# Rebuilding weight sums from copies in DRAM, two softmax units at a time, in an attention and gated-projection kernel on one Trainium2 core

## The chip, the core and the metric

The kernel runs on one core of a Trainium2 chip. The metric is the device time of one execution in microseconds (us). The engines are named as the profile names them: PE is TensorE (PEld its weight loads), DVE is VectorE, ACT is ScalarE, POOL is GpSimd, and SP is SyncE, which issues most DMAs; PEq, ACTq, SPq are the sequencers of the engines.

## The reference

Attention over 4 batches, 8 heads, 768 positions, head size 64, with a window of 128 and 4 sink positions that every row sees; then a gated projection with two weights of 512 x 1536 and one of 1536 x 512:

```python
scores = scale * np.matmul(q, k.transpose(0, 1, 3, 2))
keep = is_sink | in_window
scores = np.where(keep, scores, -1000000000.0)
scores = scores - np.max(scores, axis=-1, keepdims=True)
a = np.exp(scores)
a = a / (np.sum(a, axis=-1, keepdims=True) + 1e-09)
x = np.matmul(a, v)              # to rows of 512, 3072 of them
return (x @ w_a) * (x @ w_b) @ w_out
```

The weights arrive as 64-bit floats. The kernel computes at close to fp32 accuracy: an fp32 operand is split into a high part, rounded for fast matmuls (fp32r), and a low part, the rest; a product is three matmuls: high by high, high by low, low by high.

## The kernel before, in words

**Chunks.** The 3072 rows are done in seven chunks. The first holds the first tile of 128 rows of each batch (512 rows), the second and third the second tiles of two batches each (256 rows), and the fourth to seventh the remaining four tiles of a batch each (512 rows). While the projection of one chunk runs, the attention of the next runs beside it. In the profile, the first chunk takes about 0 to 168 us, the second to 248, the third to 322, the three following some 117 us each, the last to the end.

**First chunk (`first_tiles`, then `moe`).** Here the 36 weight tiles `w_a`, `w_b`, `w_o` (12 of each, `[128, 512]`) are loaded as 64-bit words (L340), turned into fp32 in an `io` buffer (`wf`: L347, L348 on DVE, L356 on ACT, L359 on DVE, for the first three on POOL), rounded to the high part by ACT (L371) and subtracted to the low part by DVE (L377). `moe` runs over 12 steps j: product with `w_a` (L892), copy on ACT (L927), product with `w_b`, DVE multiplication (L931), high part on ACT (L934), low part on DVE (L936), and the projection with `w_o` of the step before (L919). Beside it runs the exact attention of the second chunk: scores (L800), subtraction and maximum on DVE (L804), exponential on ACT (L806), sums (L809, L810), scaling (L811), transposes (L823), eviction of the transposed probabilities (L824), product with v (L834). In this chunk the instructions not marked by `keep_in_program_order` are ordered by the list scheduler.

**Second and third chunk (`moe2`).** The same 12 steps for 256 rows (L976 to L983), in slots: three per step, 37 calls in the second chunk. A slot runs the step's own operations, advances the attention by its pace (`PACE`), runs one stage of each piece of deferred work (`later`, `step_late`). From the second chunk on, PE, DVE, ACT and POOL keep the order in which the code was written (`begin_order`, `keep_order`); SP's DMAs don't. The attention beside the second chunk is at first the exact one of the third chunk (`apart`), then the split one for whole batches (keys and queries split on POOL, L404 and L407; scores L695; L701, L702 on DVE; exponential L704 on ACT; sums L711, L712 on DVE; scaling L713 and the copy of the sink columns L714 on ACT).

**Later chunks (`moe7`).** The products with `w_a` and `w_b` are done by halves with seven products instead of eight, which needs four sums S1 to S4 of the halves of two neighbouring tiles (2i and 2i + 1), split into high and low. These are built once, by `convert`, for i = 0 to 5 and both weights: twelve times, called rebuilds here. A rebuild adds the high and low parts of the two tiles back to fp32 (L1013, L1014), makes the four sums on POOL (L1017, L1018, L1021, L1022, each `[128, 256]`), rounds on ACT (L1025), subtracts on DVE (L1031), and sends the two results to DRAM with `send` (L1040, 512 KB each), whence `fetch` streams them in the later chunks (L1054).

**Where the rebuilds stand.** Six stand in the first chunk's steps 1 to 6 (`behind(j)`; the sums with `e = gpsimd`, their tiles in the homes of weights that come late, `LATE_HOMES`), four in the second chunk at slots 0, 8, 15 and 22 (in the tile `xh`, sums on DVE) and two in the third at slots 12 and 22 (in `w_o1`, `w_o2`):

```python
CONVERTS = {1: (0, 8, 15, 22), 2: (12, 22)}
LATE_HOMES = (("w_o11", "w_o10"), ("w_b11", "w_a11"))
return [[sums], [first], [second], [lambda: high(0)], [lambda: high(1), lambda: low(0)], [lambda: low(1)]]
```

In the split attention every unit (a head and a tile) ends on its own in `finish`, at the slot after its exponential:

```python
nc.vector.tensor_scalar(st[:, 2:3], st[:, 1:2], 1e-9, None, op0=ALU.add)
nc.vector.reciprocal(st[:, 3:4], st[:, 2:3])
nc.scalar.mul(p, p, st[:, 3:4])
nc.scalar.copy(sc[i][:, h, :], p[:, P:])
```

Other transfers that matter: keys and queries of the split attention (L427, L431), the exact attention's loads (L789 to L792), rows of the output (L1191), copies of `w_o` to DRAM (`send_o`). `io` is a ring of six buffers of `[128, 512]`.

Of the kernel before, what the change touches and what calls it, by code (L numbers as in the profile page):

```python
# [19 lines left out]
DM, FF = 512, 1536  # L20
# [217 lines left out]
class Fast:  # L238
# [419 lines left out]
    def parts_split(self, segs):  # L658
# [31 lines left out]
        def scores(h, i):  # L690
            ks, qh, ql = kq[h]
            u = f"{tag}_{h}_{i}"
            ps = self.ps.tile([P, SW], F32, tag=self.bank("s"), name=f"s{u}")
            for n, q in enumerate((qh, ql)):
                nc.tensor.matmul(ps, lhsT=q[:, i * P:(i + 1) * P], rhs=ks[:, c0s[i]:c0s[i] + SW],  # L695
                                 start=n == 0, stop=n == 1)
            if i % 2 == 0:
                state["p"] = self.at.tile([P, 2, W], F32, tag="p", name=f"p{u}")
            p = state["p"][:, i % 2, :]
            st = self.at.tile([P, 4], F32, tag="st", name=f"st{u}", bufs=8)  # L700
            nc.vector.copy_predicated(ps[:, :P], self.own.bitcast(mybir.dt.uint16), ps[:, W:])  # L701
# [3 lines left out]
            state[h, i] = p, st  # L705
            if h == 0:
                sc[i] = self.at.tile([P, H, NS], F32, tag=f"sc{i}", name=f"sc{u}", bufs=2)

        def finish(h, i):
            p, st = state[h, i]  # L710
            nc.vector.tensor_scalar(st[:, 2:3], st[:, 1:2], 1e-9, None, op0=ALU.add)  # L711
            nc.vector.reciprocal(st[:, 3:4], st[:, 2:3])  # L712
            nc.scalar.mul(p, p, st[:, 3:4])  # L713
            nc.scalar.copy(sc[i][:, h, :], p[:, P:])  # L714

        def transposes(h):
            tp = self.ps.tile([P, nt, P], F32, tag=self.bank("t"), name=f"t{tag}_{h}")
            for i in range(nt):
                nc.tensor.transpose(tp[:, i, :], state.pop((h, i))[0][:, :P], self.ident)  # L719
# [20 lines left out]
        def sinks_t():  # L740
# [3 lines left out]
            for i in range(nt):  # L744
                nc.tensor.transpose(tp[:, i * P:(i + 1) * P], sc[i].rearrange("p a b -> p (a b)"), self.ident)
# [16 lines left out]
    def parts_exact(self, segs, xf, apart):  # L762
# [56 lines left out]
        def transposes(h, i):  # L819
# [4 lines left out]
            nc.scalar.copy(ptx[:, h % 2, 2 * i:2 * i + 2, :], tp)  # L824
# [123 lines left out]
    def moe2(self, c, rows, xs, between, extra):  # L948
# [23 lines left out]
        for j in range(NJ):  # L972
# [8 lines left out]
            self.later([[lambda g=g, gh=gh: A.copy(gh, g)],  # L981
                        [lambda e=e, g=g, gh=gh, gl=gl: e.tensor_tensor(gl, g, gh.bitcast(F32), op=ALU.subtract)]])  # L982
# [13 lines left out]
    def convert(self, kind, i, homes, e):  # L996

        nc = self.nc
        (eh, el), (oh, ol) = self.wt[kind, 2 * i], self.wt[kind, 2 * i + 1]
        tag = f"{kind}{i}"  # L1000
        g, flat = nc.gpsimd, lambda x: x.rearrange("p a c -> p (a c)")
        f, h, q = None, None, None

        def sums():
            nonlocal f, h, q
            if homes is None:
                both = self.mo.tile([P, 8, HK], F32, tag="xh", name=f"s_{tag}", bufs=1)
                f, h = both[:, :4], both[:, 4:].bitcast(F32R)
            else:
                f = self.wp.tile([P, 4, HK], F32, tag=homes[0], name=f"sf_{tag}")  # L1010
                h = self.wp.tile([P, 4, HK], F32R, tag=homes[1], name=f"sh_{tag}")
            q = [f[:, k, :] for k in range(4)]
            e.tensor_tensor(flat(f[:, :2]), oh.bitcast(F32), ol.bitcast(F32), op=ALU.add)  # L1013
            e.tensor_tensor(flat(f[:, 2:]), eh.bitcast(F32), el.bitcast(F32), op=ALU.add)  # L1014

        def first():
            g.tensor_tensor(q[1], q[0], q[1], op=ALU.add)  # L1017
            g.tensor_tensor(q[0], q[2], q[0], op=ALU.subtract)  # L1018

        def second():  # L1020
            g.tensor_tensor(q[2], q[1], q[2], op=ALU.subtract)  # L1021
            g.tensor_tensor(q[3], q[3], q[2], op=ALU.subtract)  # L1022

        def high(k):
            nc.scalar.copy(flat(h[:, 2 * k:2 * k + 2]), flat(f[:, 2 * k:2 * k + 2]))  # L1025
            if k:
                self.send(("H", kind, i), flat(h).bitcast(F32))

        def low(k):
            x = flat(f[:, 2 * k:2 * k + 2])  # L1030
            nc.vector.tensor_tensor(x.bitcast(F32R), x, flat(h[:, 2 * k:2 * k + 2]).bitcast(F32), op=ALU.subtract)  # L1031
            if k:
                self.send(("L", kind, i), flat(f))

        return [[sums], [first], [second], [lambda: high(0)], [lambda: high(1), lambda: low(0)], [lambda: low(1)]]

    def send(self, key, x):
        d = self.away[key] = self.dr.tile([P, 2 * DM], F32, tag="d_" + "_".join(map(str, key)),
                                          name="d_" + "_".join(map(str, key)))
        self.nc.sync.dma_start(d, x)  # L1040
# [278 lines left out]
    def run(self, scalars, verdict):  # L1319
# [56 lines left out]
        for c in range(len(chunks) + 1):  # L1376
# [33 lines left out]
            def behind(j):  # L1410
                if 1 <= j < 7:
                    i, k = (j - 1) // 2, (j - 1) % 2
                    for part in self.convert("ab"[k], i, LATE_HOMES[k], self.nc.gpsimd):
                        for f in part:
                            f()

            def send_o(j):
                self.send(("O", j), self.whole["o", j].bitcast(F32).rearrange("p a c -> p (a c)"))

            def extra(s):  # L1420
                j, k = divmod(s, 3)
                if c == 1:
                    if s in CONVERTS[1]:
                        n = 6 + CONVERTS[1].index(s)
                        yield self.convert("ab"[n % 2], n // 2, None, self.nc.vector)
# [5 lines left out]
                if s in CONVERTS[2]:  # L1431
                    n = 10 + CONVERTS[2].index(s)
                    yield self.convert("ab"[n % 2], n // 2, ("w_o1", "w_o2"), self.nc.vector)
# [110 lines left out]
```

## Time and profile before

| | us |
|---|---|
| median of 3 runs | 782.2 (781.09 to 784.73) |
| profiled execution | 781.96 |
| its span, first to last instruction | 780.2 |
| PE busy | 738.4 (95%) |
| DVE busy | 474.9 (61%) |
| ACT busy | 415.6 (53%) |
| POOL busy | 395.5 (51%) |

A row of a table by stage gives, for a stretch of the span, the time that each engine was busy in it (and its instructions), the mean TensorE clock that was granted (PEclk, 1.00 is full speed), the mean busy share of the 16 DMA engines and what they moved. A row of a list of groups gives line, engine, operation, what is written and read, the count, then busy time and mean length of one (ns), then the idle time of the engine just before them and what ended it. In a timeline the number in brackets is the idle time before the instruction and its releaser. Lengths of overlapping instructions include the overlap.

### The profile page before, as it was taken

Reading aid. Unit: us, or ns where it says so; the run is one execution under the profiler, and the core shown is the slowest. Engines: PE = TensorE matmul, PEld = TensorE weight load, DVE = VectorE, ACT = ScalarE, POOL = GpSimd, SP = SyncE. Lnnn points to the kernel's source line nnn. Section 1 sums busy time; section 2 is a strip of 40 time slices with the busy share of each in tenths; the row PEclk is TensorE's granted clock in tenths of the full one; section 3 lists DMA queues with packets and bytes.
Section 4 is the critical chain, followed back from the end, with each engine's and each line's share of the span. In section 5 each row is a group of like instructions: output and inputs, shape, how many; then the busy total and the mean of one; then the engine's idle time right before and its main releaser. Section 6 shows DMA issues by size and latency. Waiting matters only on the chain.

```text
span 780.2 us, 14687 instructions
## 1 busy us (share of the span) xinstructions
PE 738.4 (95%) x4952; PEld 646.4 (83%) x4952; DVE 474.9 (61%) x1397; ACT 415.6 (53%) x1215; POOL 395.5 (51%) x402
## 2 busy tenths in 40 slices
PE   9887969999988999889999999999999999999997
PEld 6765748788877989888988898888898888889896
DVE  6899989945446565765564665564665664543322
ACT  6575557647646664566652476652475552444211
POOL 2646430022285673577753877753877733533340
PEclk9998989999999999999999999999999999999999
DMA  9875747535432444377876577776576765589551
GB/s 337 307 253 206 258 151 264 214 120 165 139 118 92 128 138 163 129 247 222 252 246 227 179 264 252 255 246 218 187 272 240 244 214 198 198 290 332 188 163 57
DMA packets 70275, 163.27 MB, mean 209 GB/s; under 512 B 7473, under 2 KB 24881, under 8 KB 70193
## 3 DMA queue, kind: packets, MB, share of 16 engines
q1 hardware_dynamic: 70048, 162.26, 61.8%
q8 instruction: 41, 0.67, 0.3%
q14 instruction: 42, 0.34, 0.1%
q10 hardware_dynamic: 144, 0.00, 0.0%
HBM read 138.64 MB, written 23.59 MB: 208 GB/s over the span
## 4 chain that ended last, share of the span: by engine, by line
PE 76%; DVE 8%; POOL 7%; ACT 3%; issue 3%; DMA 2%; SPq 0%; ACTq 0%; DVEq 0%; POOLq 0%
PE o L1181 15%; PE a L892 6%; PE b L892 6%; PE av L731 4%; PE s L695 4%; PE o L969 4%; PE o L919 3%; PE t L719 2%; PE X_1b L1134 2%; PE X_4b L1134 2%; PE X_2b L1134 2%; PE X_3b L1134 2%; PE s L800 2%; PE X_0b L1134 2%; PE X_4a L1134 1%
## 5 line engine op out<-in xcount | busy, mean ns | idle before, releaser
L1181 PE MATMUL o<-r_O,gh 128*128 128x512 f32 x288 | 93.7, 406 | 0.0
L1294 POOL TENSOR_TENSOR gl<-bu,gh 128x512 fp32r<-128x512 f32 x46 | 59.3, 1289 | 54.2 <-ACT gh L1291 53.3
L713 ACT ACTIVATE p<-p,st 128x132 f32<-128x132 f32 x128 | 52.0, 406 | 54.1 <-DVE st L712 53.9
L704 ACT ACTIVATE p<-p,st 128x132 f32<-128x132 f32 x128 | 51.9, 405 | 53.6 <-DVE st L702 53.1
L711 DVE TENSOR_SCALAR st<-st 128x1 f32<-128x1 f32 x128 | 19.4, 152 | 64.2 <-ACT p L704 64.2
L701 DVE COPY_PREDICATED s<-own,s 128x128 f32<-128x128 uint16 x128 | 36.9, 288 | 34.5 <-PE s L695 33.9
L1181 PE MATMUL o<-r_O,gl 128*128 128x512 f32 x144 | 56.5, 392 | 0.0
L407 POOL TENSOR_TENSOR ks<-kr,ks 64x656 fp32r<-64x656 f32 x32 | 50.9, 1592 | 2.7
L1181 PEld LDWEIGHTS o<-r_O,gh 128*128 128x128 f32 x288 | 45.0, 189 | 2.6 <-issue 2.1
L1227 POOL TENSOR_TENSOR bu<-x 128x256 f32<-128x256 f32 x24 | 19.0, 792 | 53.8 <-DVE x L1226 53.6
L919 PE MATMUL o<-w_o,gh 128*128 128x512 f32 x96 | 35.0, 436 | 9.4 <-DVE w_o L377 8.2
L721 DVE TENSOR_TENSOR pt<-t,tri 128x1024 f32<-128x1024 f32 x32 | 39.1, 1221 | 6.1 <-PE t L719 6.1
L982 POOL TENSOR_TENSOR gl<-g,gh 128x256 fp32r<-128x256 f32 x22 | 18.2, 828 | 48.4 <-ACT gh L981 48.2
L407 POOL TENSOR_TENSOR ql<-qr,qh 128x512 fp32r<-128x512 f32 x32 | 41.3, 1292 | 1.5
L892 PE MATMUL a<-x,w_a 128*128 128x256 f32 x288 | 41.0, 292 | 0.4 <-DVE x L877 0.4
L404 POOL TENSOR_SCALAR ks<-kr 64x656 fp32r<-64x656 f32 x32 | 23.9, 746 | 34.1 <-PE s L695 33.5
L695 PE MATMUL s<-ks,qh 128*128 128x260 f32 x128 | 37.9, 296 | 3.3 <-DVE st L702 2.0
L702 DVE CUSTOM_DVE_ANT_0 p<-s,mg 128x132 f32<-128x132 f32 x128 | 37.8, 296 | 4.4
L1291 ACT CAST gh<-bu 128x512 fp32r<-128x512 f32 x48 | 29.5, 614 | 19.5 <-PE o L1181 10.2
L892 PE MATMUL b<-x,w_b 128*128 128x256 f32 x288 | 39.4, 285 | 0.0
L892 PEld LDWEIGHTS a<-x,w_a 128*128 128x128 f32 x288 | 37.8, 195 | 1.3 <-DVE x L877 0.6
L695 PE MATMUL s<-ks,ql 128*128 128x260 f32 x128 | 36.6, 286 | 1.0 <-POOL ql L407 1.0
(495 smaller groups left out, 2327.4 us busy)
## 6 DMA issues: line engine op xcount, KB each, us to landing
r_O<-d_O SPq DMA_DIRECT2D x36, 512.0 KB, 4.4
r_H_a<-d_H_a SPq DMA_DIRECT2D x24, 512.0 KB, 5.2
r_L_a<-d_L_a SPq DMA_DIRECT2D x24, 512.0 KB, 6.0
r_H_b<-d_H_b SPq DMA_DIRECT2D x24, 512.0 KB, 5.0
r_L_b<-d_L_b SPq DMA_DIRECT2D x24, 512.0 KB, 5.7
qr<-in_qT_dram SPq DMA_DIRECT2D x32, 256.0 KB, 3.4
raw_a<-in_wa_dram SPq DMA_DIRECT2D x12, 512.0 KB, 6.4
raw_b<-in_wb_dram SPq DMA_DIRECT2D x12, 512.0 KB, 5.3
```

The costliest lines, as they stand in the source:

```text
L407: self.nc.gpsimd.tensor_tensor(o, i, high.bitcast(F32), op=ALU.subtract)
L695: nc.tensor.matmul(ps, lhsT=q[:, i * P:(i + 1) * P], rhs=ks[:, c0s[i]:c0s[i] + SW], start=n == 0, stop=n == 1)
L701: nc.vector.copy_predicated(ps[:, :P], self.own.bitcast(mybir.dt.uint16), ps[:, W:])
L702: nc.vector.tensor_tensor_reduce(out=p, in0=ps[:, :W], in1=self.mg[:, :W], scale=-0.125, scalar=BIG, op0=ALU.add, op1=ALU.min, accum_out=s ...
L704: nc.scalar.activation(p, p, AF.Exp, bias=st[:, 0:1], scale=-1.0, accum_out=st[:, 1:2])
L713: nc.scalar.mul(p, p, st[:, 3:4])
L721: nc.vector.tensor_tensor(self.parted(nt)[:, h % 2].rearrange("p (c m) q -> p c m q", m=2), tp.unsqueeze(2).to_broadcast(shape), self.tri. ...
L892: mm = self.nc.tensor.matmul(ps[:, cols], lhsT=w[:, ksl], rhs=x[:, kk, cols], start=start and kk == 0 and i == 0, stop=kk == NK - 1 and i ...
L919: nc.tensor.matmul(outs[i], lhsT=g[:, sl], rhs=w, start=j == 0 and k == 0, stop=j == NJ - 1 and k == 2)
L1134: mm = self.nc.tensor.matmul(ps, lhsT=a[:, ksl], rhs=b[:, kk, :], start=start and kk == 0 and n == 0, stop=kk == 1 and n == 2, skip_group_ ...
L1181: self.nc.tensor.matmul(outs[t], lhsT=g[:, sl], rhs=w, start=j == 0 and n == 0, stop=j == NJ - 1 and n == 2)
L1294: (V if late else G).tensor_tensor(hl[k][1], halves[k], hl[k][0].bitcast(F32), op=ALU.subtract)
```

## The change

1. The fp32 values of each `w_a` and `w_b` tile are stored to DRAM when the tile is made in the first chunk: 24 DMAs of 256 KB on ACT's queue, behind the high part.
2. No rebuild stands in the first chunk. Seven stand in the second (slots 0 to 24, alternately in `xh` and in four `io` buffers) and five in the third (slots 12 to 26, in tiles of `w_o`).
3. A rebuild loads the two fp32 tiles (two DMAs of 256 KB on SP) where it added high and low parts before; its POOL operations start two slots later. Its results are sent in halves: four stores of 256 KB where there were two of 512 KB.
4. In the split attention two units share a `p` and an `st` tile, and `finish` runs once for both.
5. The exact attention of the third chunk evicts the transposed probabilities on DVE where ACT did it.
6. In `moe2` the last step's low part `gl` is made in the same slot as its high part.

```diff
-CONVERTS = {1: (0, 8, 15, 22), 2: (12, 22)}
+CONVERTS = {1: ((0, "xh"), (3, "io"), (8, "xh"), (11, "io"), (16, "xh"), (19, "io"), (24, "xh")),
+            2: ((12, ("w_o1", "w_o2")), (18, ("w_o3", "w_o4")), (20, ("w_o1", "w_o2")), (23, ("w_o5", "w_o6")),
+                (26, ("w_o3", "w_o4")))}
-LATE_HOMES = (("w_o11", "w_o10"), ("w_b11", "w_a11"))
@@ weight_high
         self.tc.keep_in_program_order(self.nc.scalar.copy(w[:, 0, :], self.wf[kind, j]))
+        if kind != "o":
+            self.send(("F", kind, j), self.wf[kind, j], self.nc.scalar)
@@ parts_split: scores, finish
             if i % 2 == 0:
                 state["p"] = self.at.tile([P, 2, W], F32, tag="p", name=f"p{u}")
+                state["st"] = self.at.tile([P, 4, 2], F32, tag="st", name=f"st{u}", bufs=8)
-            st = self.at.tile([P, 4], F32, tag="st", name=f"st{u}", bufs=8)
+            st = state["st"][:, :, i % 2]
...
         def finish(h, i):
+            if i % 2 == 0:
+                return
             p, st = state[h, i]
-            nc.vector.tensor_scalar(st[:, 2:3], st[:, 1:2], 1e-9, None, op0=ALU.add)
-            nc.vector.reciprocal(st[:, 3:4], st[:, 2:3])
-            nc.scalar.mul(p, p, st[:, 3:4])
-            nc.scalar.copy(sc[i][:, h, :], p[:, P:])
+            nc.vector.tensor_scalar(st[:, 2], st[:, 1], 1e-9, None, op0=ALU.add)
+            nc.vector.reciprocal(st[:, 3], st[:, 2])
+            for k in range(2):
+                nc.scalar.mul(p[:, k, :], p[:, k, :], st[:, 3, k:k + 1])
+            nc.scalar.copy(sc[0][:, i - 1:i + 1, h, :], p[:, :, P:])
@@ parts_exact: transposes
-            nc.scalar.copy(ptx[:, h % 2, 2 * i:2 * i + 2, :], tp)
+            (nc.vector.tensor_copy if apart else nc.scalar.copy)(ptx[:, h % 2, 2 * i:2 * i + 2, :], tp)
@@ moe2
-            self.later([[lambda g=g, gh=gh: A.copy(gh, g)],
-                        [lambda e=e, g=g, gh=gh, gl=gl: e.tensor_tensor(gl, g, gh.bitcast(F32), op=ALU.subtract)]])
+            parts = [[lambda g=g, gh=gh: A.copy(gh, g)],
+                     [lambda e=e, g=g, gh=gh, gl=gl: e.tensor_tensor(gl, g, gh.bitcast(F32), op=ALU.subtract)]]
+            self.later(parts if j < NJ - 1 else [parts[0] + parts[1]])
@@ convert
-            e.tensor_tensor(flat(f[:, :2]), oh.bitcast(F32), ol.bitcast(F32), op=ALU.add)
-            e.tensor_tensor(flat(f[:, 2:]), eh.bitcast(F32), el.bitcast(F32), op=ALU.add)
+        def fetch():
+            if homes == "io":
+                f[:] = [self.io([P, 2, HK], F32, f"sf{k}_{tag}") for k in range(2)]
+                h[:] = [self.io([P, 2, HK], F32R, f"sh{k}_{tag}") for k in range(2)]
+            else:
...
+            for k in range(2):
+                nc.sync.dma_start(f[k].rearrange("p a c -> p (a c)"), self.away["F", kind, 2 * i + 1 - k])
...
+        def part(n, x, k):
...
+            nc.sync.dma_start(self.away[key][:, k * DM:(k + 1) * DM], x.rearrange("p a c -> p (a c)"))
...
-        return [[sums], [first], [second], [lambda: high(0)], [lambda: high(1), lambda: low(0)], [lambda: low(1)]]
+        return [[fetch], [], [first], [lambda: high(0), second], [lambda: high(1), lambda: low(0)], [lambda: low(1)]]
@@ run
             def behind(j):
-                if 1 <= j < 7:
-                    i, k = (j - 1) // 2, (j - 1) % 2
-                    for part in self.convert("ab"[k], i, LATE_HOMES[k], self.nc.gpsimd):
-                        for f in part:
-                            f()
+                pass
```

## Rows read from the trace of the kernel before

**Rows 1.** The page, busy time of each engine over the span

```profile
PE 738.4 (95%) x4952; PEld 646.4 (83%) x4952; DVE 474.9 (61%) x1397; ACT 415.6 (53%) x1215; POOL 395.5 (51%) x402
```

**Rows 2.** Table by stage: PE, PEld, DVE, ACT, POOL busy; PEclk, DMA share, GB/s

```profile
0.00:24.00 24.00, 22.28 (x175) 17.66 (x176) 16.35 (x54) 16.53 (x47) 5.62 (x22) 1.00 0.93 331
24.00:105.00 81.00, 64.04 (x297) 48.78 (x297) 76.75 (x132) 47.39 (x100) 47.69 (x38) 0.91 0.67 231
105.00:168.00 63.00, 63.00 (x300) 49.75 (x301) 53.30 (x118) 36.58 (x83) 0.37 (x1) 0.98 0.57 197
168.00:248.00 80.00, 75.66 (x527) 67.33 (x526) 37.92 (x149) 48.27 (x148) 38.43 (x43) 0.96 0.42 137
248.00:322.00 74.00, 69.70 (x519) 62.34 (x519) 46.01 (x147) 45.03 (x140) 42.22 (x46) 1.00 0.41 131
322.00:434.00 112.00, 109.80 (x801) 99.12 (x801) 68.25 (x237) 60.06 (x197) 69.76 (x70) 1.00 0.73 239
```

**Rows 3.** Chain of waits that ended last, 24 to 168 us: start, length, what

```profile
86.40 4.12 DMA d_L_b<-sf_b
90.67 1.81 POOL sf_b L1013
...
104.80 3.62 PE o L919 x8
```

**Rows 4.** PE's waits, 24 to 105 us: total, times, longest

```profile
PE o L919 <- DVE w_o L377: 8.2, 3, 6.3
PE s L800 <- DVE st L804: 3.8, 1, 3.8
```

**Rows 5.** Table by stage of L348, L359 (DVE, then POOL), L347 alone, in turn

```profile
24.00:105.00 81.00, 17.92 (x18) 0.91 0.67 231
105.00:165.00 60.00, 11.01 (x16) 0.97 0.60 206
...
24.00:105.00 81.00, 15.66 (x17) 3.03 (x2) 0.91 0.67 231
105.00:165.00 60.00, 11.00 (x16) 0.00 (x0) 0.97 0.60 206
...
24.00:105.00 81.00, 12.31 (x18) 0.91 0.67 231
105.00:165.00 60.00, 6.40 (x16) 0.97 0.60 206
```

**Rows 6.** Table by stage of L1031 alone (DVE)

```profile
24.00:105.00 81.00, 7.88 (x9) 0.91 0.67 231
```

**Rows 7.** ACT's timeline at the start: its only DMA issue

```profile
0.81 0.40 ACTq L1474 DMA_DIRECT2D nw_raw<-in_nw_dram  x1
```

**Rows 8.** Groups of POOL by line, 168 to 320 us: a rebuild's operation

```profile
L1018 POOL TENSOR_TENSOR s_a<-s_a 128x256 f32<-128x256 f32 x2 | 1.5, 738 | 0.2
```

**Rows 9.** The page's DMA issues: count, KB each, us from issue to landing

```profile
out_dram<-os SPq DMA_DIRECT2D x24, 256.0 KB, 2.9
```

**Rows 10.** PE's timeline in the second and third chunk

```profile
224.62 0.58 PE L695 MATMUL s<-ks,ql 128*128 128x260 f32 x1 [0.96 <-POOL ql L407]
...
244.75 0.79 PE L969 MATMUL o<-w_o,gl 128*128 128x512 f32 x1 [1.90 <-DVE gl L982]
...
283.06 0.50 PE L969 MATMUL o<-w_o,gl 128*128 128x512 f32 x1 [1.94 <-POOL gl L982]
...
320.55 0.50 PE L969 MATMUL o<-w_o,gl 128*128 128x512 f32 x1 [1.93 <-DVE gl L982]
```

**Rows 11.** Waits of SP's queue, 160 to 320 us: total, times, longest

```profile
SPq L427 <- POOL ks L407: 31.1, 4, 11.3
```

**Rows 12.** Groups by line: the split attention's sums over the span; evictions, 168 to 320 us

```profile
L711 DVE TENSOR_SCALAR st<-st 128x1 f32<-128x1 f32 x128 | 19.4, 152 | 64.2 <-ACT p L704 64.2
L712 DVE RECIPROCAL st<-st 128x1 f32<-128x1 f32 x128 | 21.1, 164 | 4.4
...
L824 ACT COPY ptx<-t 128x256 f32<-128x256 f32 x16 | 5.7, 357 | 0.1
```

More of the change, by code (lines that the diff above doesn't have):

```diff
@@ L994, in moe2, with convert @@
             self.store(outs[t], r, t, f"{c}_{t}", False)
-    def convert(self, kind, i, homes, e):
+    def convert(self, kind, i, homes):
         nc = self.nc
-        (eh, el), (oh, ol) = self.wt[kind, 2 * i], self.wt[kind, 2 * i + 1]
         tag = f"{kind}{i}"
[L1001 to L1008, printed above, removed]
-            else:
-                f = self.wp.tile([P, 4, HK], F32, tag=homes[0], name=f"sf_{tag}")
-                h = self.wp.tile([P, 4, HK], F32R, tag=homes[1], name=f"sh_{tag}")
-            q = [f[:, k, :] for k in range(4)]
-            e.tensor_tensor(flat(f[:, :2]), oh.bitcast(F32), ol.bitcast(F32), op=ALU.add)
-            e.tensor_tensor(flat(f[:, 2:]), eh.bitcast(F32), el.bitcast(F32), op=ALU.add)
+        g = nc.gpsimd
+        f, h = [], []
+        def fetch():
+            if homes == "io":
+                f[:] = [self.io([P, 2, HK], F32, f"sf{k}_{tag}") for k in range(2)]
+                h[:] = [self.io([P, 2, HK], F32R, f"sh{k}_{tag}") for k in range(2)]
+            else:
+                if homes == "xh":
+                    both = self.mo.tile([P, 8, HK], F32, tag="xh", name=f"s_{tag}", bufs=1)
+                    x, y = both[:, :4], both[:, 4:].bitcast(F32R)
+                else:
+                    x = self.wp.tile([P, 4, HK], F32, tag=homes[0], name=f"sf_{tag}")
+                    y = self.wp.tile([P, 4, HK], F32R, tag=homes[1], name=f"sh_{tag}")
+                f[:], h[:] = ([t[:, 2 * k:2 * k + 2] for k in range(2)] for t in (x, y))
+            for k in range(2):
+                nc.sync.dma_start(f[k].rearrange("p a c -> p (a c)"), self.away["F", kind, 2 * i + 1 - k])
+        q = lambda k: f[k // 2][:, k % 2, :]
@@ L1016, in first @@
         def first():
[L1017 to L1018 removed]
+            g.tensor_tensor(q(1), q(0), q(1), op=ALU.add)
+            g.tensor_tensor(q(0), q(2), q(0), op=ALU.subtract)
         def second():
[L1021 to L1022 removed]
+            g.tensor_tensor(q(2), q(1), q(2), op=ALU.subtract)
+            g.tensor_tensor(q(3), q(3), q(2), op=ALU.subtract)
@@ L1024, in high @@
+        def part(n, x, k):
+            key = (n, kind, i)
+            if key not in self.away:
+                self.away[key] = self.dr.tile([P, 2 * DM], F32, tag="d_" + "_".join(map(str, key)),
+                                              name="d_" + "_".join(map(str, key)))
+            nc.sync.dma_start(self.away[key][:, k * DM:(k + 1) * DM], x.rearrange("p a c -> p (a c)"))
         def high(k):
-            nc.scalar.copy(flat(h[:, 2 * k:2 * k + 2]), flat(f[:, 2 * k:2 * k + 2]))
-            if k:
-                self.send(("H", kind, i), flat(h).bitcast(F32))
+            nc.scalar.copy(h[k], f[k])
+            part("H", h[k].bitcast(F32), k)
@@ L1029, in low @@
         def low(k):
[L1030 to L1033, printed above, removed]
-        return [[sums], [first], [second], [lambda: high(0)], [lambda: high(1), lambda: low(0)], [lambda: low(1)]]
-    def send(self, key, x):
-        d = self.away[key] = self.dr.tile([P, 2 * DM], F32, tag="d_" + "_".join(map(str, key)),
+            nc.vector.tensor_tensor(f[k].bitcast(F32R), f[k], h[k].bitcast(F32), op=ALU.subtract)
@@ L1039, in send @@
+            part("L", f[k], k)
+        return [[fetch], [], [first], [lambda: high(0), second], [lambda: high(1), lambda: low(0)], [lambda: low(1)]]
+    def send(self, key, x, queue):
+        d = self.away[key] = self.dr.tile(list(x.shape), F32, tag="d_" + "_".join(map(str, key)),
                                           name="d_" + "_".join(map(str, key)))
-        self.nc.sync.dma_start(d, x)
+        queue.dma_start(d, x)
     def shift(self, i):
@@ L1410, in behind @@
             def behind(j):
-                if 1 <= j < 7:
-                    i, k = (j - 1) // 2, (j - 1) % 2
-                    for part in self.convert("ab"[k], i, LATE_HOMES[k], self.nc.gpsimd):
-                        for f in part:
-                            f()
+                pass
             def send_o(j):
-                self.send(("O", j), self.whole["o", j].bitcast(F32).rearrange("p a c -> p (a c)"))
+                self.send(("O", j), self.whole["o", j].bitcast(F32).rearrange("p a c -> p (a c)"), self.nc.sync)
             def extra(s):
                 j, k = divmod(s, 3)
+                for n, (at, homes) in enumerate(CONVERTS[c], len(CONVERTS[1]) * (c - 1)):
+                    if at == s:
+                        yield self.convert("ab"[n % 2], n // 2, homes)
                 if c == 1:
-                    if s in CONVERTS[1]:
-                        n = 6 + CONVERTS[1].index(s)
-                        yield self.convert("ab"[n % 2], n // 2, None, self.nc.vector)
                     if k == 0 and j < KEPT:
```

13 lines of the change are left out of this document (5 added, 8 removed).

## The prediction

> **What bounds the kernel now.** I read the page first: TensorE (PE) is busy for 738.4 of 780.2 us, so the whole kernel can give back little more than 42 us of idle PE, plus what PE loses at a lower clock [rows 1]. The table by stage says where those 42 us lie: 17.0 of them between 24 and 105 us, inside the first chunk, where the granted clock averages 0.91. From 105 to 168 us PE has no gap. The second and third chunk lose 4.3 us each, and the stage from 322 to 434 us, which stands for three alike, loses 2.2 [rows 2].
>
> The chain of waits then says what PE waits for from 24 to 105 us. It runs through VectorE (DVE) and through GpSimd (POOL), which rebuilds weight sums there: a store of an earlier rebuild (4.1 us) lets POOL start L1013 at 90.7 us, then come eleven POOL operations one after another, and PE goes on at 104.8 us [rows 3]. In the list of PE's waits the low halves of w_o (L377, on DVE) cost 8.2 us and one wait for the score subtraction on DVE 3.8, together 12.0 of the 17.0 [rows 4]. The stage table shows that DVE is busy for 76.75 of these 81 us: it is DVE that is late.
>
> Why DVE is late is seen by putting its lines in the two stretches side by side. L348 takes 17.92/18 = 1.00 us in the first and 11.01/16 = 0.69 in the second, L359 0.92 against 0.69, L347 0.68 against 0.40 [rows 5]. The operations are the same; what differs is POOL, busy for 47.69 us in the first stretch and 0.37 in the second [rows 2]. [...]
>
> **The change, part by part.**
>
> *The first chunk loses six rebuilds.* On DVE this removes the twelve subtractions of L1031; those before 105 us are busy for 7.88 us [rows 6]. On POOL it removes 36 operations, nearly all of the 47.69 us; two sums at L359 stay on POOL (3.03 us) [rows 5]. Without them the three DVE lines come back to their undisturbed length: 18 x 0.31 + 17 x 0.23 + 18 x 0.28 = 14.5 us. So DVE is relieved by 7.9 + 14.5 = 22.4 us of 81, other lines not counted. PE can take at most its idle time and its lost clock: 17.0 + 0.09 x 81 = 7.3, together 24.3. I take less. The 8.2 us for w_o go whole. The 3.8 us come early, beside the two POOL sums that stay, so half: 1.9. The other 5.0 are small waits of the same kind: half, 2.5. Of the 7.3 us of clock I take the share of idle time that goes (12.6/17.0) and of time in which PE was busy (64.04/81): 4.3. That is 16.9. PE is the bound after that, as it is from 105 us on, where DVE is busy for 53.30 of 63 us including what is left of L1031.
>
> *Added there:* 24 stores of 256 KB, issued by ScalarE (ACT) behind the high halves. Nothing new is waited for, since the copy ahead of each store has waited for the same tile. The one DMA issue on ACT in this trace takes 0.40 us [rows 7], so 24 cost 9.6 us on an engine that is busy for 47.39 of 81 us and loses twelve casts. That is cover enough; I charge 1 us of later weights. What would break the cover is a longer issue: with 47.4 + 36.6 us of ACT work left in the 128 us to which 144 would shrink, 24 issues have 44 us, or 1.8 us each. The bytes are those of the twelve removed 512 KB stores. If the stretch shrinks from 81 to 65 us its 231 GB/s become 288, under the 331 that the first 24 us moved [rows 2], so transfers don't bound it. Sum for this chunk: **16 us**, between 8 (only L1031 counts) and 24.
>
> *The second and third chunk gain six rebuilds*, now 7 and 5, each with a load (two of 256 KB) in place of two DVE sums. Per added rebuild POOL gets 4 operations of 0.74 us [rows 8], so 3 x 4 x 0.74 = 8.9 us per chunk, on 38.43 of 80 and 42.22 of 74 busy; ACT gets two casts, DVE two subtractions, and all twelve rebuilds together lose the sums. PE covers this as long as nobody queues. The engines run these stages in a fixed order, so one late operand holds what stands behind it: if the load is late, POOL's first operation waits, behind it the subtractions of gl and the key and query splits, and PE behind those. The load has two slots, 2 x 80/37 = 4.3 us; a 256 KB transfer lands in 2.9 us [rows 9]. A stall of this kind stands in the trace: at 283.06 us PE waited 1.94 us for a gl which POOL did behind a rebuild [rows 10]. Upper price for a stall: 1.9 plus some 1.5 us at half clock, since the second chunk's clock of 0.96 loses 3.2 us over its two groups of stalls; lower price zero, if the other queue has the slack. I charge two added stalls at 1.9, less the one removed: 2.
>
> SyncE gets 24 loads and twice as many, half as large, stores: 48 more issues, by the row of 0.40 us some 19 us of a queue over 154 us. The queue stands in order behind loads of keys that wait for POOL (31.1 us in four waits, one of 11.3) [rows 11]; a load of a rebuild that comes behind one is late by that much. This is what the second rival is made of.
>
> The transfers of these two chunks move 137 and 131 GB/s at shares of 0.42 and 0.41. Three more rebuilds stored (3.1 MB) and seven loaded (3.7 MB) make 222 in the second, less in the third; 239 passes at a share of 0.73 from 322 us on [rows 2]. So I cost them at nothing. [...]
>
> *The last gl of each moe2 one slot earlier.* At 244.75 and 320.55 us PE waits 1.90 and 1.93 us for exactly this subtraction on DVE [rows 10]. It now follows its high half at once, ahead of the work of a further slot. Both go: 3.8, between 0 (the gh copy is then late) and 5.3 with the clock behind the first.
>
> *Sums of two units at once.* Of 128 additions (L711, 0.152 us) and 128 reciprocals (0.164) half go [rows 12]: 64 x 0.316 = 20 us of DVE, and 64 copies on ACT. Late in the second chunk the chain runs through these. But PE has few gaps there beyond those already counted, and 2.2 us per later stage. The stall at 224.62 us (0.96) [rows 10] waits for a query split on POOL, with half a rebuild ahead of it; that rebuild moves to other slots: 1 us. For three later chunks: 0.5 in all, between 0 and 5, since their gaps belong to POOL and to the change of batch.
>
> *Sixteen evictions on DVE in place of ACT* (0.357 us there) [rows 12]: 5.7 us onto a DVE with 37.92 of 80 us busy, beside a PE that is busy for 75.66 [rows 2]. Nothing; at most 1 us if DVE were late.
>
> **Sum:** 16 + (3.8 + 1 - 2 = 2.8) + 0.5 = 19.3 us. The profiled execution took 781.96 us, 0.2 under the median of 782.2, so 762.7; I say **763**.
>
> **Rivals.**
> *A, DVE stays the pace-maker.* Each step needs three weights of four DVE operations, and the order of the first chunk is not written out by hand for these lines; without the rebuilds it can come out with less lead. Then only L1031 counts, 8 us: 782 - 8 = **774**. For it: DVE is busy for 53 of 63 us even undisturbed. Against: PE had no gap there.
>
> *B, rebuilds stall the second and third chunk.* Loads stand late in SyncE's queue, POOL waits, gl and the queries come late. Price 3.4 us (1.9 and the clock); from seven of twelve rebuilds on it eats 19.3 + 3.9 us, at nine the time is 782 - 19.3 + 30.6 = **793**. For it: the waits of 11.3 us in that queue. Against: five of twelve are over before the keys' splits begin, with POOL nearly idle, and the queue already sends stores of w_o long before their slot.
>
> *C, given back:* B with about six rebuilds: 782 - 19.3 + 20.4 = **783**.
>
> **How the numbers follow.** Forecast 0.76, A 0.12, C 0.05, B 0.07. A measurement of this kernel tells about 0.5% (3.9 us) from no change. Forecast and A are faster by more: 0.88; C is the same: 0.05; B slower: 0.07. The low end is 24.3 + 5.3 + 1 us off: 751. The high end is A with nothing for the last gl and the two stalls that I charge: 782 - 8 + 2 = 776. The range is **751 to 776**; it leaves out C and B, 0.12.
>
> **What would show it.** After: PE's clock near 1.00 and under 6 us idle up to the end of the first chunk, which ends near 152 us and not 168; DVE's L348 at 0.69 us throughout; POOL all but idle there; L711 64 times; no wait for gl where the second and third chunk end; no chain through a rebuild's load. I am wrong if POOL waits on landings of these loads, if DVE waits for the new stores to release its tiles, or if ACT shows long gaps at its issues.

## The result and the profile after

The changed kernel takes 763.0 us (median of 4 runs, 759.96 to 764.34) against 783.1 (781.09 to 784.73) for the kernel before in the same sitting: a ratio of 0.974 [0.970, 0.978]. The forecast was 763. That the number is met does not make its terms right. The first chunk gave 5 us more than its term, the later chunks gave nothing, and one sentence of the working left out a cost of some 5 us.

The starts of the first output copy of each chunk (L1206 on ACT; L1190 before) cut the two profiled executions, of 759.96 and 781.96 us, into chunks:

| chunk | before, us | after, us | gained | the forecast's term |
|---|---|---|---|---|
| first | 167.7 | 146.7 | 21.0 | 16 |
| second and third | 153.4 | 151.6 | 1.8 | 2.8 |
| fourth to the end | 459.1 | 459.9 | -0.8 | 0.5 |
| span | 780.2 | 758.2 | 22.0 | 19.3 |

Lines of after lie one to seven further down than those of before in these parts: L348 became L349, L359 L360, L711 L717, L712 L718, L919 L926, L969 L976, L982 L989. In kernels with the single finish, below, those from L720 on lie three higher again (L973 for L976, L986 for L989, L1026 for L1029); in e_cols, which has a line more, the addition is L718.

The page of after, busy time of each engine over the span, answers to [rows 1]:

```profile
PE 730.9 (96%) x4952; PEld 642.9 (85%) x4952; DVE 466.6 (62%) x1273; ACT 391.6 (52%) x1135; POOL 370.5 (49%) x390
```

The table by stage of after, with the columns of [rows 2] and stages cut at its own chunk ends:

```profile
0.00:24.00 24.00, 20.46 (x150) 15.18 (x151) 14.21 (x47) 13.67 (x41) 4.18 (x20) 1.00 0.93 337
24.00:105.00 81.00, 79.47 (x413) 65.90 (x413) 74.47 (x179) 57.68 (x127) 4.40 (x3) 0.98 0.94 333
105.00:146.00 41.00, 41.00 (x204) 32.66 (x203) 31.90 (x66) 22.51 (x49) 0.00 (x0) 1.00 0.33 109
146.00:226.00 80.00, 75.27 (x540) 66.75 (x538) 44.56 (x155) 45.95 (x133) 47.88 (x55) 1.00 0.66 216
226.00:300.00 74.00, 71.43 (x526) 63.40 (x527) 51.25 (x129) 46.00 (x137) 53.22 (x58) 1.00 0.66 210
300.00:428.00 128.00, 124.54 (x897) 112.08 (x897) 79.44 (x228) 61.24 (x199) 85.09 (x84) 1.00 0.70 228
```

From 24 to 105 us PE now has 1.5 us without work where it had 17.0, at a granted clock of 0.98 where it was 0.91, and POOL is nearly still (4.40 us, not 47.69). But the first 24 us became worse: PE is busy for 20.46 us there, not 22.28. The table by stage of L349 alone (DVE) shows why the middle became better; it answers to the first lines of [rows 5]:

```profile
24.00:105.00 81.00, 17.16 (x25) 0.98 0.94 333
105.00:146.00 41.00, 6.21 (x9) 1.00 0.33 109
```

That is 0.69 us for each of 25, where before it was 1.00 for each of 18. What is left of PE's waits from 24 to 105 us is short (one more of 0.3 us), and is no longer the wait for w_o of [rows 4]:

```profile
PE afirst L899 <- ACT xh L573: 1.2, 1, 1.2
```

At the ends of the second and third chunk, PE's timeline of after answers to [rows 10]:

```profile
221.75 0.73 PE L976 MATMUL o<-w_o,gh 128*128 128x512 f32 x2 [1.64 <-ACT gh L988]
...
226.78 0.96 PE L899 MATMUL a<-x,w_a 128*128 128x256 f32 x3 [1.47 <-ACT x L883]
...
295.73 0.51 PE L976 MATMUL o<-w_o,gl 128*128 128x512 f32 x1 [0.25 <-DVE gl L989]
```

In the third chunk the wait for gl shrank from 1.93 to 0.25 us, as forecast. In the second PE now waits for gh and then for x, both from ACT: 3.1 us where gl had cost 1.90. PE's waits for POOL in the two chunks (total, times, longest) are short:

```profile
PE s L698 <- POOL ql L410: 1.8, 2, 0.9
PE o L976 <- POOL gl L989: 0.6, 1, 0.6
```

Last, ACT's timeline after the start. The second number is the length, and DMA_DIRECT2D at L1056 is one of the new stores of the fp32 copies:

```profile
20.60 0.33 ACTq L1056 DMA_DIRECT2D d_F_a<-wf_a  x1
21.04 1.15 ACT L530 ACTIVATE p<-s,st 128x128 f32<-128x128 f32 x4 [1.98 <-DVE v L555]
...
31.90 0.33 ACTq L1056 DMA_DIRECT2D d_F_a<-wf_a  x1
32.27 0.59 ACT L573 CAST xh<-xt 128x512 fp32r<-128x512 f32 x1 [1.77 <-POOL wf_a L360]
```

Neither store stands behind its cast. The scheduler put them ahead, and the exponentials and the cast of xh that follow don't use that tile at all. ACT sat idle for 1.98 and 1.77 us before them, and PE after that:

```profile
22.71 2.05 PE L551 MATMUL av<-v,pt 128*128 128x128 f32 x16 [1.63 <-ACT pt L540]
32.91 0.38 PE L899 MATMUL afirst<-xh,w_a 128*128 128x256 f32 x1 [1.18 <-ACT xh L573]
```

### The profile page after: what moved, and what is told of

Same layout as the page of the kernel before. It is cut to its first block, busy times and chain, and to the rows that moved or that the text cites. A ratio compares the mean times of both kernels' runs of the same rounds, so it can differ in the third digit from the quotient of the medians.

```text
span 758.2 us, 14626 instructions
## 1 busy us (share of the span) xinstructions
PE 730.9 (96%) x4952; PEld 642.9 (85%) x4952; DVE 466.6 (62%) x1273; ACT 391.6 (52%) x1135; POOL 370.5 (49%) x390
## 4 chain that ended last, share of the span: by engine, by line
PE 78%; POOL 7%; DMA 6%; DVE 3%; ACT 3%; issue 2%; SPq 1%; ACTq 0%; POOLq 0%; DVEq 0%
PE o L1197 15%; PE b L899 7%; PE a L899 7%; PE o L926 4%; PE av L738 4%; PE s L698 4%; PE o L976 2%; PE s L807 2%; PE X_1b L1150 2%; PE X_4b L1150 2%; PE X_3b L1150 2%; PE t L726 2%; PE X_0b L1150 2%; PE X_4a L1150 2%; PE X_2a L1150 2%
## 5 line engine op out<-in xcount | busy, mean ns | idle before, releaser
L708 ACT ACTIVATE p<-p,st 128x132 f32<-128x132 f32 x128 | 51.7, 404 | 82.2 <-DVE st L706 82.0
L720 ACT ACTIVATE p<-p,st 128x132 f32<-128x132 f32 x128 | 44.9, 398 | 39.6 <-DVE st L718 39.6
L1029 POOL TENSOR_TENSOR s_a<-s_a 128x256 f32<-128x256 f32 x4 | 2.9, 734 | 123.2 <-PE o L926 114.2
L717 DVE TENSOR_SCALAR st<-st 128x2 f32<-128x2 f32 x64 | 36.3, 567 | 42.5 <-ACT p L708 42.5
L1307 ACT CAST gh<-bu 128x512 fp32r<-128x512 f32 x48 | 29.4, 613 | 19.5 <-PE o L1197 10.2
L899 PEld LDWEIGHTS b<-x,w_b 128*128 128x128 f32 x288 | 36.2, 189 | 0.4 <-issue 0.3
```

The source lines that it names most:

```text
L717: nc.vector.tensor_scalar(st[:, 2], st[:, 1], 1e-9, None, op0=ALU.add)
L720: nc.scalar.mul(p[:, k, :], p[:, k, :], st[:, 3, k:k + 1])
L899: mm = self.nc.tensor.matmul(ps[:, cols], lhsT=w[:, ksl], rhs=x[:, kk, cols], start=start and kk == 0 and i == 0, stop=kk == NK - 1 and i ...
```

## The experiments

They are told in the order of the questions. A kernel that has no edit named here is the changed one. Chunk times are cut as above.

**Was it POOL, or DVE's own work? (e_pool, e_dve)** e_pool puts the POOL part of the six old rebuilds back into the first chunk, e_dve only twelve DVE subtractions in the place of those of L1031. Both are extra work whose results nobody reads.

```diff
             def behind(j):
-                pass
+                if 1 <= j < 7:
...
+                    g.tensor_tensor(flat(f[:, :2]), oh.bitcast(F32), ol.bitcast(F32), op=ALU.add)
+                    g.tensor_tensor(flat(f[:, 2:]), eh.bitcast(F32), el.bitcast(F32), op=ALU.add)
+                    g.tensor_tensor(q[1], q[0], q[1], op=ALU.add)
...
```

In e_dve the body is two `nc.vector.tensor_tensor(..., op=ALU.subtract)` of the size of L1031.

> The changed kernel with the POOL part of the six removed rebuilds put back into the first chunk (36 operations, into tiles that nobody reads): no subtractions on DVE, no casts on ACT, no stores, and nothing waits for their results but the loads of w_o11 and w_b11. It adds work whose results are not used. Theory (POOL's work stretches DVE's operations, and DVE is what PE waits for): L348 goes from 0.69 back to about 1.0 us beside it, the first chunk ends 12 to 18 us later (at 161 to 167 us, not 148.8), the time is 775 to 781 us. Rival (the gain came from the removed DVE subtractions and from DVE and ACT no longer waiting for POOL's results): nothing waits here, so the time stays within 2 us of 763.

> The changed kernel with twelve subtractions of 128x512 on DVE put into the first chunk where the rebuilds were (results unused), 12 x 0.6 = 7.2 us of DVE, and no POOL work. Theory (contention is most of the gain, and DVE has a little room once POOL is quiet): 0 to 4 us more than the changed kernel, 763 to 767 us. Rival (the removed subtractions were the gain): 8 us or more, 771 us and over.

e_pool: 777.0 us (776.46 to 780.09), ratio 0.992 [0.989, 0.995]; the first chunk ends at 165.3 us, 18.6 later than in after. e_dve: 765.8 (763.35 to 766.35), ratio 0.977 [0.974, 0.980]; the first chunk ends at 150.5, 3.8 later. The table by stage of e_pool, then that of its L349 alone:

```profile
24.00:105.00 81.00, 67.47 (x333) 53.00 (x334) 73.20 (x135) 47.70 (x104) 45.10 (x39) 0.97 0.78 265
...
24.00:105.00 81.00, 19.34 (x19) 0.97 0.78 265
105.00:146.00 41.00, 9.32 (x14) 1.00 0.66 233
```

With POOL busy for 45.10 us, L349 is back at 19.34/19 = 1.02 us, and still 0.67 where POOL has stopped. PE again waits for low halves made on DVE, 9.8 us in these two rows of its list from 24 to 165 us:

```profile
PE o L926 <- DVE w_o L380: 5.3, 4, 2.0
PE b L899 <- DVE w_b L380: 4.5, 5, 1.4
```

From 105 us on its only wait is 0.8 us, so the tiles that the added work takes from the last weights hold nothing up. By the medians 14 of the 20 us that the change brings are POOL's work (18.6 of 21.0 in the profiled first chunks), not through what it makes but through what it does to DVE beside it. DVE's own subtractions are 2 to 4. In both kernels PE's wait for pt near 23 us is longer as well (4.6 and 3.2 us, where after has 1.6), ahead of the first added operation; in e_cols, below, it is 3.7, and the first chunk ends at 146.8 all the same, so it explains little of the 18.6.

**The stores on ACT (e_spstore, e_pin).** e_spstore issues the 24 stores on SP. e_pin leaves them on ACT, but holds each behind its cast in the order of the code.

```diff
@@ weight_high, in e_spstore
-            self.send(("F", kind, j), self.wf[kind, j], self.nc.scalar)
+            self.send(("F", kind, j), self.wf[kind, j], self.nc.sync)
@@ send, in e_pin
-        queue.dma_start(d, x)
+        op = queue.dma_start(d, x)
+        if queue is self.nc.scalar:
+            self.tc.keep_in_program_order(op)
```

> The changed kernel with the 24 stores of fp32 copies issued on SP in place of ACT. The prediction charged 1 us for 24 issues on ACT. Theory (they lie beside other work): within 2 us of 763. Rival (issues on ACT cost as much as 24 x 0.4 = 9.6 us of the first chunk): 753 to 757 us. If SP's queue, in order behind weight loads, is the worse place, over 765 us.

> The changed kernel with each of the 24 stores kept on ACT but held in program order behind its cast. With the stores on SP the first chunk ended 5 us earlier. In the changed kernel the store of the first tile stands ahead of exponentials that do not need it, and ACT stood idle for 2 us there, and for 1.8 us at the third store; both wait for sums on POOL. Theory (the place in ACT's queue costs, not the issue): 757 to 760 us, the first chunk ends at 142 to 144 us. Rival (24 issues on ACT cost, 0.33 us and more each): 762 to 764 us, no change.

e_spstore: 756.8 us (755.47 to 758.89), ratio 0.967 [0.964, 0.970], first chunk to 141.7. e_pin: 757.2 (756.52 to 759.99), ratio 0.968 [0.965, 0.970], first chunk to 143.6. In the profiled first chunks that is 5.0 us back for e_spstore and 3.2 for e_pin; the six runs that leave first chunk and stores as in after end theirs between 146.4 and 146.8. The rest of the 6 to 7 us between the medians lies behind the first chunk and is not traced to the stores. The issues themselves are the same 24 in e_pin, so most of the cost is their place in ACT's queue, not their number. It does not show in PE's idle time alone: for the same 767 matmuls PE is idle for 5.1 us of the first chunk in after, 5.9 in e_pin and 2.1 in e_spstore, and busy for 141.7, 137.6 and 139.6, at a mean clock from 24 to 105 us of 0.98, 1.00 and 1.00. ACT's timeline of e_pin:

```profile
21.30 0.67 ACT L372 CAST w_a<-wf_a 128x512 fp32r<-128x512 f32 x1
23.47 0.34 ACTq L1056 DMA_DIRECT2D d_F_a<-wf_a  x1
23.85 1.07 ACT L540 COPY pt<-t 128x512 f32<-128x512 f32 x2 [1.89 <-DMA vx<-in_vB_dram]
...
26.91 0.62 ACT L372 CAST w_b<-wf_b 128x512 fp32r<-128x512 f32 x1 [0.94 <-POOL wf_b L360]
26.91 0.34 ACTq L1056 DMA_DIRECT2D d_F_b<-wf_b  x1
```

The exponentials and the first cast of xh now stand ahead of the first store. Yet that store still holds ACT: the cast ends at 21.97 and the issue comes at 23.47. The tile cannot be what it waits for. The chain of waits of after says the same of its first store:

```profile
11.46 9.07 DMA raw_a<-in_wa_dram
20.53 0.02 issue
20.55 0.02 ACTq L1056
20.57 0.04 issue
20.60 0.33 ACTq L1056
```

It puts the store behind the landing of a load issued at 11.46, the third of raw_a, while the first tile's sum on POOL was over at 17.63 + 1.29 = 18.92. Why a store should depend on that load is not shown. With the stores on SP no arithmetic of ACT stands behind them, and in e_spstore PE is again busy for 22.33 of the first 24 us; in e_pin, where the first store still holds ACT, for 19.66.

**Two units at once (e_single, e_cols).** In the changed kernel L717 appears in the profile with a length it did not have. One line on each kernel's addition, minimum/median/maximum in ns, after first, then e_cols:

```profile
L717 DVE TENSOR_SCALAR st<-st x64: 164/394/1505, 205.6 to 618.1; 128x2 f32<-128x2 f32 x64
```

```profile
L718 DVE TENSOR_SCALAR st<-st x128: 136/150/157, 206.6 to 617.7; 128x1 f32<-128x1 f32 x128
```

The forecast took 0.152 us for it [rows 12]. Two timelines of after, DVE's and POOL's, show when it is long:

```profile
329.36 0.79 DVE L717 TENSOR_SCALAR st<-st 128x2 f32<-128x2 f32 x1 [0.56 <-ACT p L708]
...
335.10 0.17 DVE L717 TENSOR_SCALAR st<-st 128x2 f32<-128x2 f32 x1 [0.57 <-ACT p L708]
...
340.42 1.22 DVE L717 TENSOR_SCALAR st<-st 128x2 f32<-128x2 f32 x1 [0.57 <-ACT p L708]
```

```profile
328.53 1.59 POOL L410 TENSOR_TENSOR ks<-kr,ks 64x656 fp32r<-64x656 f32 x1
...
340.01 1.60 POOL L410 TENSOR_TENSOR ks<-kr,ks 64x656 fp32r<-64x656 f32 x1
```

The first ends at 330.15 and POOL's operation at 330.12, the third at 341.64 and POOL's at 341.61. Where POOL is idle, at 335.10, it takes 0.17 us. Of the 64 additions 36 take over 0.2 us, and each of these ends within 0.1 us of the end of a POOL operation. So in after the addition of two columns waited for the POOL operation in progress to end, up to 1.505 us; none of the 128 additions of one column in e_cols took over 0.157 us. e_single has the four lines of the old finish again, on the slices of the shared tiles; e_cols keeps the pair and does the addition column by column.

```diff
@@ finish, in e_single
-            if i % 2 == 0:
-                return
-            p, st = state[h, i]
+            p, st = state[h, i][0][:, i % 2, :], state[h, i][1][:, :, i % 2]
-            nc.vector.tensor_scalar(st[:, 2], st[:, 1], 1e-9, None, op0=ALU.add)
+            nc.vector.tensor_scalar(st[:, 2:3], st[:, 1:2], 1e-9, None, op0=ALU.add)
...
@@ finish, in e_cols
-            nc.vector.tensor_scalar(st[:, 2], st[:, 1], 1e-9, None, op0=ALU.add)
+            for k in range(2):
+                nc.vector.tensor_scalar(st[:, 2, k:k + 1], st[:, 1, k:k + 1], 1e-9, None, op0=ALU.add)
```

> The changed kernel with the split attention's sums taken one unit at a time again (the pair tiles stay). The trace after shows the addition for two units at 0.57 us in the mean and not 0.15, ending where a POOL operation ends. Theory (this addition waits for POOL, off PE's path): DVE's additions take 0.15 us again, and the time moves by less than 2 us either way, 761 to 765. Rival (pairing shortened the chain and is a real part of the gain): 3 to 6 us slower, 766 to 769, lost in the second chunk and at the changes of chunk.

> The changed kernel with the addition for two units done as two additions of one column; the rest of the pairing stays. Theory (an addition of two columns on DVE waits until a running POOL operation ends, one of one column does not): each addition takes 0.15 us also beside POOL, DVE is busy some 17 us less in all, and the time falls by 1 to 3 us, 760 to 762, as with single units. Rival (the long addition comes from the strided read or from waiting for ACT): the additions stay long or the time stays at 763.

e_single: 760.4 us (757.92 to 760.55), ratio 0.971 [0.968, 0.973]; e_cols: 759.3 (757.81 to 761.91), ratio 0.970 [0.968, 0.973]. By chunks, the fifth and sixth, whose lengths hardly vary, take 117.8 and 116.4 us in after, 117.2 and 115.4 in e_single, 117.2 and 115.5 in e_cols, 117.1 and 115.7 before; the two together take 233.8 to 234.3 us in all eight profiled runs with the two-column addition and 232.6 to 232.9 in the six without it. So the pair costs some 1.4 us there, through its two-column addition alone. The fourth chunk varies by 2 us among runs of either kind (128.6 to 130.6), so its share is not settled. By what step the addition reaches PE is not shown either: in the fifth chunk PE is idle for 1.4 us in after and in e_single, and it is PE's busy time for the same 834 matmuls that differs, 116.4 against 115.8. Both medians lie below the range that was expected, by 0.6 and 0.7 us.

**The other parts (after_again, e_gl, e_evict).** after_again is the changed kernel once more. e_gl makes the last gl in its own, later step again; e_evict gives the sixteen evictions back to ACT.

```diff
@@ moe2, in e_gl
-            self.later(parts if j < NJ - 1 else [parts[0] + parts[1]])
+            self.later(parts)
@@ transposes, in e_evict
-            (nc.vector.tensor_copy if apart else nc.scalar.copy)(ptx[:, h % 2, 2 * i:2 * i + 2, :], tp)
+            nc.scalar.copy(ptx[:, h % 2, 2 * i:2 * i + 2, :], tp)
```

> The changed kernel once more, beside the next three, so that a difference of 1 to 3 us can be told: 763 us, within 1.5.

> The changed kernel with the last low part gl of the second and third chunk made one slot after its high part again. The prediction gave this part 3.8 us. The trace after shows PE waiting 1.64 us for the high part at the end of the second chunk and 0.25 for gl at the end of the third. Theory (part of it was won): 764 to 766 us. Rival (the wait only changed its name): 763, within 0.5.

> The changed kernel with the sixteen evictions of exact attention on ScalarE again. The prediction costed this part at nothing: 763.5 us, within 1 us. If ScalarE sets the end of the second chunk after the change (PE waits there for gh and for x, both on ScalarE), 16 x 0.36 = 5.7 us more ScalarE work makes the second and third chunk up to 2 us longer each: 766 to 767.

after_again: 763.9 us (762.51 to 765.05), ratio 0.976 [0.973, 0.978]. e_gl: 760.1 (759.53 to 761.91), ratio 0.971 [0.969, 0.973]. e_evict: 760.6 (758.89 to 762.21), ratio 0.971 [0.968, 0.973]. Undoing either part makes the kernel no slower; by the medians it is 2 to 4 us faster, below every value that was expected. That is not seen in the work: the second and third chunk take 151.5 to 151.6 us in the profiled runs of after, e_gl and e_evict alike, and e_evict's list of PE's waits has the entries of after's within 0.1 us. The timeline of e_gl has the old waits back, 0.92 and 1.93 us for gl, and the wait for x down to 0.33 from 1.47. The wait for gh is the same as in after, so the earlier gl did not make it:

```profile
221.71 0.73 PE L976 MATMUL o<-w_o,gh 128*128 128x512 f32 x2 [1.64 <-ACT gh L988]
```

What differs is the granted clock: its mean is 0.993 to 0.998 over the five executions of e_gl, 0.991 to 0.997 over those of e_evict and 0.991 to 0.995 over those of after_again. The table by stage of after_again, then of after, same stretches:

```profile
228.00:230.00 2.00, 2.00 (x13) 2.00 (x13) 1.13 (x4) 0.87 (x3) 1.59 (x2) 0.63 0.84 273
230.00:232.00 2.00, 2.00 (x11) 1.37 (x11) 1.75 (x6) 0.93 (x4) 1.33 (x2) 0.52 0.93 325
```

```profile
228.00:230.00 2.00, 2.00 (x18) 1.78 (x19) 1.39 (x4) 0.71 (x3) 1.85 (x2) 1.00 0.96 292
230.00:232.00 2.00, 2.00 (x24) 1.48 (x19) 1.50 (x6) 1.18 (x5) 1.08 (x2) 1.00 0.89 306
```

The same program, with waits of 1.64 us for gh and 1.47 to 1.48 for x ahead of it in both, was granted a clock of 0.63 and 0.52 over these 4 us in one execution and of 1.00 in the other. By these shares (1 - 0.63 + 1 - 0.52) x 2 = 1.7 us are lost. In before, the table by stage has the half clock of the forecast from 246 to 248 us, behind the wait of 1.90 us of [rows 10]: 0.50. Over the four executions of after, time and clock go together: 759.96 at 0.996, 762.6 at 0.993, 763.42 at 0.991, 764.34 at 0.989. So single profiles of this kernel can differ by 1 to 4 us with no change of the work, and two of my parts are smaller than that.

**Put together (e_sp_single, e_sp_single_gl, e_sp_single_early).** e_sp_single joins e_spstore and e_single (the sums finished singly are those of the split attention). The other two add e_gl's edit, or begin the second chunk's rebuilds earlier:

```diff
@@ CONVERTS, in e_sp_single_early
-CONVERTS = {1: ((0, "xh"), (3, "io"), (8, "xh"), (11, "io"), (16, "xh"), (19, "io"), (24, "xh")),
+CONVERTS = {1: ((0, "xh"), (3, "io"), (7, "xh"), (10, "io"), (14, "xh"), (17, "io"), (21, "xh")),
```

> The stores of the weight copies go out on SyncE, and the sums of exact attention are finished one unit at a time as before. If the two costs found so far (the place of the stores in ScalarE's queue, about 6 us in the first chunk; the two-column addition behind POOL, about 3 us in the last four chunks) lie in different stages and don't overlap, they add up: 763.5 - 6.5 - 3 = 754 us (752 to 756), the first chunk ends near 142 us and the fourth takes at most 129.5. If the gain of the single finish was only another course of the same kernel (execution to execution 1 to 3 us), it stays at the 756.8 of the stores alone.

> The same kernel with the last low half of gates (gl) in its own, later step, as in the kernel before. The prediction's 3.8 us for the earlier step would make this 754 + 3.8 = 758. The theory that the earlier step only renames the wait (PE waits for gh on ScalarE and x where it waited for gl) gives 754, within 1 us of the kernel beside it. If the later step truly helped, as its first run hints, 751.

> As the first kernel of this call, with the seven rebuilds of the second chunk begun at steps 0, 3, 7, 10, 14, 17, 21 in place of 0, 3, 8, 11, 16, 19, 24, so that the last one's POOL work and stores are over before the keys' and queries' splits. If those stalls belong to the rebuilds (the second rival's mechanism, some 2.4 us of waits for POOL and a late load of keys), the second chunk is 2 us shorter: 752 us. If POOL's own splits set them, or the loads come late in the closer steps, nothing or a loss of 1 to 3 us: 754 to 757.

e_sp_single: **754.6 us** (753.89 to 754.92), ratio 0.963 [0.961, 0.965], the best of all and clear of the changed kernel; its first chunk ends at 140.8. Stores (763.0 - 756.8 = 6.2) and single finish (2.2 more) add up nearly as expected. e_sp_single_gl: 756.8 (754.75 to 759.91), ratio 0.966 [0.964, 0.969]. Here the later gl is 2.2 us the slower one, with overlapping intervals, where e_gl was 3.9 the faster: that part is worth nothing that these runs can settle.

e_sp_single_early missed every outcome written down, the nearest by 1.1 us: 758.1 us (757.23 to 761.91), ratio 0.968 [0.966, 0.971], and in its profiled run, the slowest of five, the second chunk takes 84.5 us, not 80.4. Its POOL timeline, PE's timeline and the table by stage:

```profile
195.98 0.72 POOL L1026 TENSOR_TENSOR s_a<-s_a 128x256 f32<-128x256 f32 x1 [5.85 <-DMA qr<-in_qT_dram]
197.46 0.72 POOL L986 TENSOR_TENSOR gl<-g,gh 128x256 fp32r<-128x256 f32 x1
```

```profile
198.24 0.50 PE L973 MATMUL o<-w_o,gl 128*128 128x512 f32 x1 [2.48 <-POOL gl L986]
201.29 0.58 PE L698 MATMUL s<-ks,qh 128*128 128x260 f32 x1 [1.86 <-POOL qh L407]
```

```profile
200.00:206.00 6.00, 3.94 (x16) 3.65 (x17) 1.92 (x6) 1.33 (x4) 5.58 (x7) 0.57 0.27 89
```

POOL stands idle for 5.85 us at the first operation of a rebuild until a transfer lands (its releaser is given as the load of queries, which the kernel issues on SP like the rebuild's own load), the gl behind it is late, PE waits for gl and then for the queries' high part, and the clock falls to 0.57. This is the second rival of the forecast, built by moving five rebuilds by one to three slots.

## Why the forecast was right, point by point

**The first chunk: mechanism right, 16 us too small.** "16 us" should have been 21.0 (21.2 in after_again). For the same 767 matmuls PE is idle for 18.7 us of the first chunk before and for 5.1 after, 13.6 less, where I had taken 12.6; and it is busy for 149.0 and then for 141.7 us, 7.3 less, where I had taken 4.3 for the clock. So the mis-sized term is the clock: PE got back 3 us more than the share that I allowed, and the 1 us charged for the stores lies within these two numbers. Some of that clock stood where I had not looked, from 105 us on (0.98 before, 1.00 after). With the stores on SP the chunk gives 26.0, so the 24.3 that I called the most was also too low. DVE is still busy for 74.47 of 81 us, and PE has no wait for its weights there; rival A (774, DVE stays the pace-maker) is refuted, and so is its premise that only L1031 counts, since e_dve puts those back for 2 to 4 us, and e_pool the rest for 14.

**"Nothing new is waited for, since the copy ahead of each store has waited for the same tile": wrong.** The sentence assumed that the store stays behind the copy. In this chunk the instructions that are not marked are placed by the scheduler, as the kernel's description says, and two of the first stores went ahead of exponentials and casts. The issue itself was what I took it for (0.33 us against 0.40). The price was 5.0 us of the first chunk by e_spstore, 3.2 of it the place by e_pin. I had charged 1 us and had written down the sign of being wrong ("long gaps at its issues"), and the trace shows it.

**Second and third chunk: 2.8 forecast, 1.8 in one execution and -0.4 in the other** (153.4 against 153.8 in after_again). The transfers held: 216 and 210 GB/s, against the 222 that I estimated for the second, and 256 KB loads landed in 3.5 to 4.4 us. The two added stalls of 1.9 us did not come about: PE's waits for POOL in the second chunk sum to 2.4 us, none over 0.94, against 2.25 before (1.29 for a query's high part and the 0.96 of [rows 10]), and the 1.94 at 283.06 is gone. So for PE's waits for POOL the terms 1 and -2 forecast a loss of 1 us, and 1.8 was won. The rival's mechanism shows in small, in the chain of waits of after, where SP's queue had a store that waited for L1048 ahead of a load of keys, and PE then waited for POOL for 0.94 us:

```profile
191.90 1.99 DVE s_a L1048 x2
193.90 0.32 SPq L1041
194.31 3.37 DMA kr<-in_kT_dram
197.68 0.08 issue
197.76 0.78 POOL ks L407
```

Another step that failed is "Both go: 3.8" for the last gl. In the third chunk 1.7 us went. In the second PE waits for gh and x on ACT, 3.1 us against 1.90: gl was not the only late operand there, and by e_gl the wait for gh is there with the later gl too. At the two ends the waits sank by 1.1 us, not 3.8 (4.4 with gh and x before, 3.4 now), and a wait of 0.9 us for a scaled p (L720, ACT) is new. That 1.8 is near 2.8 is luck: one term erred by 2.8 us up and another by 2.7 down. Rivals B and C did not happen; e_sp_single_early shows B's mechanism at a price of some 4 us.

**Later chunks: 0.5 gained forecast, 0.8 to 1.4 lost** (459.9 and 460.5 against 459.1). "Half go" was right for the reciprocals. The additions went from 128 x 0.152 = 19.5 us to 36.3 (64 x 0.567), because a wider form met POOL, to which the term gave no price; undoing it gives some 1.4 us in the fifth and sixth chunk.

**Evictions: 0 forecast, and nothing seen in the stages.** That the sum came out at 19.3 against 20.1 by the medians is luck. In after_again, whose 762.5 us is nearer the median, +5.2 us in the first chunk and -5.1 elsewhere cancelled; in the profiled execution of after, the fastest of its four, +5.0 and -2.3.

## What to carry to other kernels

An engine whose results nobody needs soon can still set the time, through the engine beside it, as in e_pool, where POOL's unused work took L349 from 0.69 to 1.02 us and cost 14 us: compare the length of the same instruction beside the neighbour and without it before its busy share is believed. A DMA issue put on a computing engine's queue can hold what stands behind it there, as the first store held ACT for 1.98 us; where a scheduler orders that queue, say where the issue stands, or give it to a queue with no arithmetic. Before merging two small vector operations into a wider one, look at what runs on the other engine: here 64 long ones took 36.3 us and 128 short ones 19.4.

## What the runs showed of the hardware that I had not expected

In after the two-column fp32 addition on DVE waited until the running POOL operation ended (0.17 us where POOL was idle, up to 1.505), while its one-column form (0.136 to 0.157 in e_cols) and the two-column reciprocal after it (0.165 to 0.168 in after and e_cols) did not. After the same waits of 1.6 and 1.5 us the granted clock fell to 0.63 and 0.52 in one execution and stayed at 1.00 in another. Open stay what the first store on ACT waits for beyond its tile, and whether the later gl or the evictions on ACT make such a fall rarer.
